# Turning the second batch's probabilities on VectorE instead of TensorE, and a table of 34 shifted due times

## The chip, the cores and the metric

The kernel runs on one core of a Trainium2 chip. The metric is the device time of one execution in microseconds (us); the figure of a kernel is the median of three runs. All parts of this document speak of that one core.

## What is computed

A causal attention over 4 batches, 12 heads, 448 positions and a head size of 64 feeds a gated feed-forward layer. Cut to what matters:

```python
def _attn_ref(q, k, v):                    # [4, 12, 448, 64], float32
    scores = np.matmul(q, k.transpose(0, 1, 3, 2)) / np.sqrt(64)
    scores = np.where(mask, -1000000000.0, scores)          # causal
    scores = scores - np.max(scores, axis=-1, keepdims=True)
    attn = np.exp(scores)
    attn = attn / (np.sum(attn, axis=-1, keepdims=True) + 1e-09)
    return np.matmul(attn, v)

def _moe_ref(x, w_gate, w_val, w_out):     # x [1792, 768], w_gate, w_val [768, 1536], w_out [1536, 768]
    gate = 1.0 / (1.0 + np.exp(-(x @ w_gate)))
    return gate * (x @ w_val) @ w_out
```

## The kernel before

**The work.** The heads are taken in pairs: six pairs for each batch, 24 in all. A pair is loaded (`load`, `load_v`), its scores are computed on TensorE, the row minimum, exponential, sum and division follow on VectorE, ScalarE and GpSimd, and the probabilities, which have the query in the partition, are turned so that the key is in the partition. The turned tile `pt` is then multiplied by V, and the result is split in a high and a low part (`features`). A batch's six results are the input of the feed-forward layer. Batches 0 and 1 go through it one by one ("units" 0 and 1, `unit_items`, matmuls at L600, three of them for each product of 128 rows, since every operand is a high and a low part); batches 2 and 3 go through it together at the end (`pair_items`, L813, the "pair stage").

**Two ways to turn a pair.** The narrow way (`score`, `trans`, `pv`) cuts queries in blocks of 112: 8 score matmuls (L283), 20 transposes on TensorE against an identity (L334), five evictions of the PSUM result into `pt` (L343 on ScalarE, L345 on VectorE; for batch 1 all five on ScalarE) and 8 matmuls with V (L358). The wide way (`wscore`, `shift`, `wpv`) cuts queries in blocks of 128: 8 score matmuls (L405), then VectorE turns 32x32 blocks within their quarter of the partitions (seven operations at L455, one at L458), and two transfers bring the blocks to the right quarter: one writes the tile to a DRAM buffer `pd` (L463, 1 MB), four read it back into `pt` (L466, a quarter each). 20 matmuls with V follow (L483). A constant, `WIDE`, tells how many batches are narrow: batches 0 and 1 before. In the wide way the tile that VectorE writes is a part of `room`, the buffer that also takes the loads of the weights in unit 0.

**Weights.** In unit 0 each of the 36 weight tiles comes from the input as 64-bit words (L565, into one of three parts of `room`), ScalarE and VectorE make float32 of it (L569, L571, L573), it is written to DRAM for later use (L576), and ScalarE and a second engine split it in a high and a low part (L581, and L583 on VectorE for 34 of the 36 tiles). In unit 1 a tile is read back from DRAM (L578) and split by ScalarE and GpSimd. Three buffers at each step (`room`, `wr`, and the high and low parts) let the loads run ahead of TensorE.

**What sets the order.** Every step is an operation of a plan (`Plan.op`) with an engine, a cost and a due time. The main loop runs through the feed-forward products in their order and drops attention steps between them at fixed fractions of the way; the due time is a running sum of costs. `Plan.order` first pulls the due time of each operation forward to that of its successors, then lists the operations engine by engine: of those that are ready, the one with the earliest due time goes first. The engines execute the lists in order. All DMAs are issued by SyncE (SP), also in the order of the list.

Of the kernel before, what the change touches and what calls it, by code (L numbers as in the profile page):

```python
# [8 lines left out]
F32 = mybir.dt.float32  # L9
# [10 lines left out]
PTW = 2 * 10 * QB  # L20
# [7 lines left out]
HP = H // 2  # L28

LAG = 1  # L30
WIDE = 2
PAIR = 2
TURN, SPREAD = 0.95, 0.85
ORDER = "1256743"
# [1 line left out]
EARLY = 2  # L36
WC = 512
EV = ((1, 3, 4), (0, 1, 2, 3, 4), (1, 3, 4), (1, 3, 4))
BUFS = dict(w64=3, wd=2, wr=3, ws=3, sm=4, raw=3, pt=3, gt=5, vr=2, st=4)
LAT, LOOK, SLACK = 0.04, 0.06, 0.2  # L40
AFTER = dict(DVE=0.09, ACT=0.1, PL=0.03)

REBIAS, SIGN = 2.0 ** -112, 2.0 ** 32


class Buf:
# [35 lines left out]
class Plan:  # L84
# [60 lines left out]
    def order(self):  # L145
        for o in reversed(self.ops):
            d = min((s.due - s.cost - SLACK for s in o.succs), default=1e9) - o.extra
            o.due = d if o.due is None else min(o.due, d)
        free = {}
        shared = 0.0  # L150
        queue = {}
        for o in self.ops:
            o.left = len(o.preds) + len(o.after)
            o.ready = 0.0
            queue.setdefault(o.eng, [])
            free[o.eng] = 0.0
            if not o.left:
                queue[o.eng].append(o)
        done = []
        while True:  # L160
            best = None
            for e, q in queue.items():
                if q:
                    t = max(free[e], min(o.ready for o in q))
                    if best is None or t < best[0]:
                        best = (t, e)
            if best is None:
                break
            t, e = best
            q = queue[e]  # L170
            o = min((o for o in q if o.ready <= t + LOOK), key=lambda o: (o.due, o.n))
            q.remove(o)
            start = max(t, o.ready, shared if o.lock else 0.0)
            end = start + o.cost
            if o.lock:
                shared = end
            free[e] = end
            done.append((start, o.n, o))
            for s in o.succs:
                s.left -= 1  # L180
                s.ready = max(s.ready, end + o.extra + (LAT if s.eng != e or e != "PE" else 0.0))
                if not s.left:
                    queue[s.eng].append(s)
            for s in o.then:
                s.left -= 1
                s.ready = max(s.ready, start)
                if not s.left:
                    queue[s.eng].append(s)
        assert len(done) == len(self.ops)
        done.sort(key=lambda x: x[:2])  # L190
        return [o for _, _, o in done]
# [3 lines left out]
def kernel(  # L195
# [7 lines left out]
    nc = tc.nc  # L203
    plan = Plan()
# [10 lines left out]
    dma = lambda b: b / 355e3 + 0.03  # L215
# [11 lines left out]
    def part(n, i):  # L227

        lo = i * n
        p = Part(room, lo, n, Gone([q for q in parts if q.lo < lo + n and lo < q.lo + q.n]))  # L230
        parts.append(p)
        return p
# [212 lines left out]
    def shift(n):  # L445

        j = pairs[n]
        j["pt"] = pt = new("pt", [128, PTW], F32, BUFS["pt"])
        tb = part(4 * WC, n % 2)
        tv = lambda: tb.t.rearrange("p (r n) -> p r n", r=4)  # L450
        plan.op("PL", 0.2, lambda: nc.gpsimd.memset(tv()[:, 2:4, WC - 32:WC], 0.0), [], [(tb, "zero")])
        for z, i in [(z, i) for i in range(3) for z in range(2)] + [(0, 3)]:
            sm, o, c, at = j["sm"][z], woff(i), min(i + 1, 3), z * 192 + ioff(i) if i < 3 else 384
            r = [(sm, (i, z))] if i < 3 else [(sm, (i, 0), (i, 1))]
# [4 lines left out]
            out=tv()[:, 0:2, WC - 32:WC],  # L459
            in_=sm.t[:, woff(3) + 384:woff(3) + 448].rearrange("p (r j) -> p r j", j=32)),  # L460
            [(j["sm"][0], (3, 0), (3, 1))], [(tb, "end")])
        pd = new("pd", [128, 4 * WC], F32, 2, bass.MemoryType.DRAM)
        plan.op("SP", dma(128 * 4 * WC * 4), lambda: nc.sync.dma_start(out=pd.t, in_=tb.t),  # L463
                [(tb, "zero", "end", *[(z, i) for z in range(2) for i in range(3)], (0, 3))], [(pd,)], extra=4.2)
        for r in range(4):
            plan.op("SP", dma(32 * 4 * WC * 4), lambda r=r: nc.sync.dma_start(  # L466
# [41 lines left out]
    def att_steps(seq, wide):  # L508

        L = []  # L510
        for m in range(len(seq) + LAG + 1):
            n, c, d = (seq[e] if 0 <= e < len(seq) else None for e in (m, m - LAG, m - LAG - 1))
            if n is not None:
                L.append((0, lambda due, n=n: load(n)))
# [182 lines left out]
    def pair_inputs():  # L697
# [7 lines left out]
                halves(xa[k], *T[p, i])  # L705
        rest = {p: [] for p in "56743"}
        for p, tags in (("5", (("raw", 2),) * 3), ("6", (("sm", 2),) * 3), ("7", (("pt", 5), ("vr", 1))),
                        ("4", (("pt", 5),)), ("3", (("pt", 5),))):
            for tag, n in tags:
                rest[p] += cells(tag, n, F32R, BUFS[tag])  # L710
        a, b = cells("sm", 2, F32R, BUFS["sm"])
# [293 lines left out]
    now -= 3.0  # L1005
    last = [PAIR * HP + k for k in range(HP)] + [(PAIR + 1) * HP + k for i in range(KH) for k in (i, KH + i)]
    att = []
    for seq, wide, lo, hi in ((range(HP, 2 * HP), False, 0.0, TURN), (last, True, TURN, 1 + SPREAD)):
        steps = att_steps(seq, wide)
        pace = [a[-1] if len(a) == 3 else a[0] for a in steps]  # L1010
        da = 0.0
        for (c, f, *_), w in zip(steps, pace):
            att.append((c, f, half * (lo + (hi - lo) * da / sum(pace))))
            da += w
# [27 lines left out]
def _lay(q, k, v, moe_w_gate, moe_w_val, moe_w_out):  # L1042
# [2 lines left out]
    qkt = np.concatenate([q.transpose(0, 1, 3, 2), k.transpose(0, 1, 3, 2)], axis=3).reshape(B * HP, 128, 2 * S)  # L1045
    vt = np.zeros((B * HP, 128, NB, 2, D), v.dtype)
    vp = v.reshape(B * HP, 2, S, D)
    m = WIDE * HP
    vt[:m, :QB] = vp[:m].reshape(m, 2, NB, QB, D).transpose(0, 3, 2, 1, 4)
    for c in range(NB):  # L1050
        x = vp[m:, :, WQ * c:WQ * c + WQ]
# [34 lines left out]
```

## Time and profile before

| | before |
|---|---|
| median of three runs | 653.56 us (653.43 to 654.2) |
| the profiled execution | 654.04 us, its span 652.3 us, granted clock 0.994 |
| TensorE busy | 642.1 us (98%) |
| VectorE, ScalarE, GpSimd busy | 445.5, 359.4, 323.3 us |
| DMA, mean over the span | 210 GB/s |

The profile takes all its times from the start of the span; 1.7 us of the execution lie outside it. Four stretches are told apart below: the opening with batch 0's attention (0 to 62 us), unit 0 with batch 1's attention (62 to 223), unit 1 with the attention of batches 2 and 3 (223 to 417), and the pair stage. "DMA share" is the mean share of time in which the 16 DMA engines were busy. The names of the engines in the rows: PE is TensorE, PEld its weight load, DVE is VectorE, ACT is ScalarE, POOL is GpSimd, SP is SyncE.

### The profile page before, as it was taken

Reading aid. Unit: us, or ns where it says so; the run is one execution under the profiler, and the core shown is the slowest. Engines: PE = TensorE matmul, PEld = TensorE weight load, DVE = VectorE, ACT = ScalarE, POOL = GpSimd, SP = SyncE. Lnnn points to the kernel's source line nnn. Section 1 sums busy time; section 2 is a strip of 40 time slices with the busy share of each in tenths; the row PEclk is TensorE's granted clock in tenths of the full one; section 3 lists DMA queues with packets and bytes.
Section 4 is the critical chain, followed back from the end, with each engine's and each line's share of the span. In section 5 each row is a group of like instructions: output and inputs, shape, how many; then the busy total and the mean of one; then the engine's idle time right before and its main releaser. Section 6 shows DMA issues by size and latency. Waiting matters only on the chain.

```text
span 652.3 us, 10853 instructions
## 1 busy us (share of the span) xinstructions
PE 642.1 (98%) x3726; PEld 539.9 (83%) x3726; DVE 445.5 (68%) x999; ACT 359.4 (55%) x815; POOL 323.3 (50%) x352
## 2 busy tenths in 40 slices
PE   6999999999999999999999999999999999999997
PEld 4566887888888778778787899999999999999997
DVE  4776987878774376556565975647764459999852
ACT  6887777767664456555465645443343434556520
POOL 3751653241520277577666766756665657700300
PEclk9899999999999999999999999999999999999999
DMA  7379599877886369998989895767532322344321
GB/s 269 120 243 327 193 305 324 264 262 260 275 295 227 118 216 270 296 303 258 280 277 293 242 308 186 227 243 242 178 114 78 114 76 73 121 134 152 98 80 70
DMA packets 46678, 137.15 MB, mean 210 GB/s; under 512 B 5152, under 2 KB 8736, under 8 KB 45088
## 3 DMA queue, kind: packets, MB, share of 16 engines
q1 hardware_dynamic: 46624, 136.47, 64.0%
q8 instruction: 29, 0.48, 0.3%
q14 instruction: 25, 0.20, 0.1%
HBM read 99.48 MB, written 36.96 MB: 209 GB/s over the span
## 4 chain that ended last, share of the span: by engine, by line
PE 95%; DMA 2%; ACT 2%; SPq 0%; DVE 0%; POOL 0%; issue 0%; DVEq 0%
PE m L600 40%; PE m L813 19%; PE s L813 10%; PE t L813 7%; PE t L334 4%; PE s L283 4%; PE m L358 3%; PE m L483 3%; PE s L405 3%; DMA raw<-in_qkt_dram 2%; ACT sm L300 1%; PE t L405 1%; PE s L358 1%; POOL wl L583 0%; SPq L466 0%; ACT sm L426 0%
## 5 line engine op out<-in xcount | busy, mean ns | idle before, releaser
L767 POOL TENSOR_TENSOR wl<-room,wh 128x384 fp32r<-128x384 f32 x84 | 96.7, 1174 | 55.2 <-ACT wh L766 55.0
L600 PE MATMUL m<-xh,wh 128*128 128x448 f32 x288 | 109.8, 381 | 0.0
L600 PE MATMUL m<-xh,wl 128*128 128x448 f32 x288 | 105.3, 365 | 0.0
L600 PE MATMUL m<-xl,wh 128*128 128x448 f32 x288 | 105.2, 365 | 0.0
L583 POOL TENSOR_TENSOR wl<-wr,wh 128x768 fp32r<-128x768 f32 x38 | 74.4, 1961 | 54.0 <-ACT wh L581 53.4
L321 POOL TENSOR_SCALAR sm<-sm,r 112x112 f32<-112x112 f32 (+1 forms) x92 | 62.6, 701 | 77.4 <-DVE r L308 71.4
L581 ACT CAST wh<-wr 128x768 fp32r<-128x768 f32 x72 | 59.6, 830 | 30.7 <-PE m L600 19.6
L600 PEld LDWEIGHTS m<-xh,wh 128*128 128x128 f32 x288 | 54.1, 188 | 20.3 <-issue 13.3
L766 ACT CAST wh<-room 128x384 fp32r<-128x384 f32 x84 | 39.6, 512 | 54.2 <-POOL wl L767 15.9
L426 ACT ACTIVATE sm<-sm,mn 128x128 f32<-128x128 f32 (+3 forms) x84 | 43.9, 524 | 43.3 <-DVE mn L420 43.3
L600 PEld LDWEIGHTS m<-xh,wl 128*128 128x128 f32 x288 | 54.1, 188 | 4.5
L600 PEld LDWEIGHTS m<-xl,wh 128*128 128x128 f32 x288 | 54.2, 188 | 3.7
L300 ACT ACTIVATE sm<-sm,mn 112x112 f32<-112x112 f32 (+3 forms) x96 | 49.8, 521 | 9.8 <-DVE mn L296 9.4
L600 PE MATMUL m<-gh,wh 128*128 128x448 f32 x144 | 53.9, 374 | 0.0
L441 POOL TENSOR_SCALAR sm<-sm,r 128x256 f32<-128x256 f32 (+3 forms) x84 | 42.7, 525 | 21.7 <-DVE r L436 12.4
L583 DVE TENSOR_TENSOR wl<-wr,wh 128x768 fp32r<-128x768 f32 x34 | 36.2, 1065 | 24.2 <-ACT wh L581 23.9
L600 PE MATMUL m<-gh,wl 128*128 128x448 f32 x144 | 52.6, 366 | 0.0
L600 PE MATMUL m<-gl,wh 128*128 128x448 f32 x144 | 52.6, 365 | 0.0
L455 DVE STREAM_TRANSPOSE room<-sm 128x384 f32<-128x384 f32 (+2 forms) x84 | 35.1, 448 | 19.1 <-POOL sm L441 17.9
L630 POOL TENSOR_TENSOR gl<-gt,gh 128x448 fp32r<-128x448 f32 x24 | 30.4, 1268 | 34.2 <-ACT gh L629 34.2
L813 PE MATMUL m<-pt,wh 128*128 128x448 f32 x150 | 44.7, 366 | 0.0
L420 DVE CUSTOM_DVE_ANT_0 sm<-s,mask 128x128 f32<-128x128 f32 (+1 forms) x72 | 29.2, 440 | 21.5 <-PE s L405 20.9
(165 smaller groups left out, 1488.9 us busy)
## 6 DMA issues: line engine op xcount, KB each, us to landing
room<-in_wp_dram SPq DMA_DIRECT2D x36, 768.0 KB, 6.6
wr<-wdram SPq DMA_DIRECT2D x45, 384.0 KB, 5.0
room<-wdram SPq DMA_DIRECT2D x45, 384.0 KB, 3.6
wdram<-wr SPq DMA_DIRECT2D x36, 384.0 KB, 7.1
pd<-room SPq DMA_DIRECT2D x12, 1024.0 KB, 6.9
pt<-pd SPq DMA_DIRECT2D x48, 256.0 KB, 5.7
raw<-in_qkt_dram SPq DMA_DIRECT2D x23, 448.0 KB, 6.2
vr<-in_vt_dram SPq DMA_DIRECT2D x24, 256.0 KB, 6.1
```

The source lines that it names most:

```text
L300: plan.op("ACT", act(ne, 0, 1) + 0.01, lambda z=z, sm=sm, i=i, ne=ne, off=off: nc.scalar.activation(out=sm.t[:QB, off:off + ne], in_=sm.t[ ...
L321: plan.op("PL", 0.24 + w / 1200, lambda args=args: nc.gpsimd.tensor_scalar(**args()), [(r_,)], [(sm, a)])
L426: plan.op("ACT", act(ne, 0, 1) + 0.01, lambda z=z, sm=sm, i=i, ne=ne, off=off: nc.scalar.activation(out=sm.t[:, off:off + ne], in_=sm.t[:, ...
L441: plan.op("PL", 0.24 + w / 1200, lambda sm=sm, i=i, o=o, w=w, z=z: nc.gpsimd.tensor_scalar(out=sm.t[:, o:o + w], in0=sm.t[:, o:o + w], sca ...
L455: plan.op("DVE", dve(128 * c) + 0.03, lambda sm=sm, i=i, o=o, c=c, at=at: nc.vector.transpose(out=tv()[:, :, at:at + 32 * c].rearrange("p ...
L581: plan.op("ACT", act(768), lambda: nc.scalar.copy(hi_.t, t.t), [(t,)], [(hi_,)])
L583: plan.op(eng, cost, lambda: at.tensor_tensor(out=lo_.t, in0=t.t, in1=hi_.t.bitcast(F32), op=ALU.subtract), [(t,), (hi_,)], [(lo_,)], lock ...
L600: nc.tensor.matmul(out=ps.t[:, :S], lhsT=a.t[:, k, :], rhs=b.t if isinstance(b, Buf) else b(), start=(first and z == 0), stop=(last and z ...
L630: plan.op("PL", 1.11, lambda: nc.gpsimd.tensor_tensor(out=gl.t[:, jj], in0=gg.t, in1=gh.t.bitcast(F32), op=ALU.subtract), [(gg,), (gh,)], ...
L766: plan.op("ACT", act(w), lambda: nc.scalar.copy(f(hi_.t), x()), [(src, at)], [(hi_, e)])
L767: plan.op("PL", 0.97, lambda: nc.gpsimd.tensor_tensor(out=f(lo_.t), in0=x(), in1=f(hi_.t).bitcast(F32), op=ALU.subtract), [(src, at), (hi_ ...
L813: nc.tensor.matmul(out=ps.t[:, :S], lhsT=a.t[:, kw, :], rhs=b.at, start=bool(first and z == 0), stop=bool(last and z == 2), skip_group_che ...
```

## The change

The six pairs of batch 1 now go the wide way: `WIDE` counts pairs and is 6, and the plan's list of attention sequences has the wide form for pairs 6 to 11. While batch 1 is worked on, `room` is full of weights, so for these pairs VectorE writes into a buffer of its own, `tb`, of which there is one; the number of `pt` buffers falls from 3 to 2 to make room for it, and the operand tiles of product "3" in the pair stage, which used a `pt` buffer, use `tb`. `NUDGE` adds a time to the due time of 34 operations after the due times have been pulled forward. V is laid out for the wide form from pair 6 on.

```diff
-WIDE = 2
+WIDE = 6
...
-BUFS = dict(w64=3, wd=2, wr=3, ws=3, sm=4, raw=3, pt=3, gt=5, vr=2, st=4)
+BUFS = dict(w64=3, wd=2, wr=3, ws=3, sm=4, raw=3, pt=2, gt=5, vr=2, st=4, tb=1)
...
+NUDGE = {
+    21: 2.7, 40: -0.7, 42: 1.8, 69: -0.8, 288: 3.1, 289: 3.1, 399: 2.1, 405: 2.1, 414: 2.1, 415: 2.1, 452: 2.1,
...
+}
...
+        for n, x in NUDGE.items():
+            self.ops[n].due += x
...
-        tb = part(4 * WC, n % 2)
-        tv = lambda: tb.t.rearrange("p (r n) -> p r n", r=4)
+        tb = part(4 * WC, n % 2) if j["b"] >= PAIR else new("tb", [128, PTW], F32)
+        at_ = lambda: tb.t[:, :4 * WC]
+        tv = lambda: at_().rearrange("p (r n) -> p r n", r=4)
...
-        plan.op("SP", dma(128 * 4 * WC * 4), lambda: nc.sync.dma_start(out=pd.t, in_=tb.t),
+        plan.op("SP", dma(128 * 4 * WC * 4), lambda: nc.sync.dma_start(out=pd.t, in_=at_()),
...
-                        ("4", (("pt", 5),)), ("3", (("pt", 5),))):
+                        ("4", (("pt", 5),)), ("3", (("tb", 5),))):
...
-    for seq, wide, lo, hi in ((range(HP, 2 * HP), False, 0.0, TURN), (last, True, TURN, 1 + SPREAD)):
+    for seq, wide, lo, hi in ((range(HP, WIDE), False, 0.0, 0.03), (range(WIDE, 2 * HP), True, 0.03, TURN), (last, True, TURN, 1 + SPREAD)):
...
-    m = WIDE * HP
+    m = WIDE
```

In the rows below the changed kernel's lines stand nine or ten higher: L414, L465, L473, L476 and L493 are the wide form's L405, L455, L463, L466 and L483 of before, L575 and L586 are L565 and L576, L610 is L600.

SyncE's list in unit 0, at the loads of the 11th to 14th weight before and the 13th to 16th now (`room<-in_wp_dram` is a weight's load, `wdram<-wr` its write back, `raw` the queries and keys of a pair, `vr` its values). Before:

```order
L565 DMA room<-in_wp_dram 128x1536
L576 DMA wdram_1343<-wr 128x768
L565 DMA room<-in_wp_dram 128x1536
L576 DMA wdram_1381<-wr 128x768
L263 DMA vr<-in_vt_dram 128x512
L565 DMA room<-in_wp_dram 128x1536
L576 DMA wdram_1426<-wr 128x768
```

Now:

```order
L575 DMA room<-in_wp_dram 128x1536
L586 DMA wdram_1195<-wr 128x768
L473 DMA pd<-tb 128x2048
L575 DMA room<-in_wp_dram 128x1536
L586 DMA wdram_1270<-wr 128x768
L266 DMA raw<-in_qkt_dram 128x896
L476 DMA pt<-pd 32x4x512 x4
L575 DMA room<-in_wp_dram 128x1536
```

A pair's write to `pd` and its four reads now stand between the loads of weights, six times between the 13th load and the last.

TensorE's list in unit 0, at a step of a pair; the L600 rows between are feed-forward products of which one is shown. Before:

```order
L358 MATMUL m<-pt,vr 64x448 x2
L358 MATMUL m<-pt,vr 64x336 x2
L358 MATMUL m<-pt,vr 64x224 x2
L358 MATMUL m<-pt,vr 64x112 x2
L283 MATMUL s<-raw 112x112 x2
L283 MATMUL s<-raw 112x224 x2
L600 MATMUL m<-xh_679,wh 128x448
...
L334 MATMUL t<-ident,sm 112x112 x4
L283 MATMUL s<-raw 112x336 x2
L334 MATMUL t<-ident,sm 112x112 x4
...
L283 MATMUL s<-raw 112x448 x2
L334 MATMUL t<-ident,sm 112x112 x8
```

Now:

```order
L493 MATMUL m<-pt,vr 64x128 x12
L493 MATMUL m<-pt,vr 64x64 x8
L414 MATMUL s<-raw 64x448 x2
L610 MATMUL m<-xh_764,wh 128x448
...
L414 MATMUL s<-raw 128x128 x2
L414 MATMUL s<-raw 128x256 x2
L414 MATMUL t<-raw 128x384 x2
```

The transposes (L334) of batch 1 are gone, 120 in all; a pair's step is scores and one burst with V.

VectorE's list in unit 0 now, beside the next weights (L581, L583 and L593 are L571, L573 and L583 of before, L637 is the gate of a feed-forward tile); before, only the weights and the softmax of a pair stood here:

```order
L465 STREAM_TRANSPOSE tb<-sm 128x4x32
L465 STREAM_TRANSPOSE tb<-sm 128x2x4x32 x2
L593 TENSOR_TENSOR wl<-wr,wh 128x768
L465 STREAM_TRANSPOSE tb<-sm 128x3x4x32
L581 TENSOR_SCALAR wr<-wd 128x768
L465 STREAM_TRANSPOSE tb<-sm 128x3x4x32
L583 SCALAR_TENSOR_TENSOR wr<-room,wr 128x768
L465 STREAM_TRANSPOSE tb<-sm 128x3x4x32
L468 STREAM_TRANSPOSE tb<-sm 128x2x32
```

The eight block transposes of a pair are interleaved with the conversion of the next weight.

## Rows read from the trace of the kernel before

**Rows 1.** Windows by stage; busy PE, PEld, DVE, ACT, POOL, clock, DMA share, GB/s.
```profile
62.00:223.00 161.00, 161.00 (x898) 132.41 (x896) 117.80 (x211) 107.42 (x220) 55.54 (x63) 1.00 0.77 260
223.00:417.00 194.00, 192.97 (x1342) 159.69 (x1339) 125.77 (x412) 105.59 (x270) 130.84 (x146) 1.00 0.83 257
572.00:652.30 80.30, 76.70 (x377) 70.35 (x375) 57.81 (x86) 33.27 (x56) 7.12 (x5) 1.00 0.31 106
```

**Rows 2.** Windows of the feed-forward matmuls (L600): length, PE busy (count), clock, DMA.
```profile
62.00:223.00 161.00, 126.58 (x588) 1.00 0.77 260
223.00:417.00 194.00, 143.29 (x674) 1.00 0.83 257
```

**Rows 3.** Chain that ended last, in order of time: start, length, what.
```profile
103.38 0.91 PE t L334 x8
...
168.18 2.04 PE m L358 x16
...
277.49 1.93 PE m L483 x40
...
395.41 22.08 PE m L600 x108
```

**Rows 4.** Windows of score matmuls: L283 up to 62, L405 up to 223.
```profile
0.00:62.00 62.00, 20.83 (x108) 9.84 (x108) 0.94 0.67 232
...
62.00:223.00 161.00, 0.54 (x6) 0.52 (x8) 1.00 0.77 260
```

**Rows 5.** DMA issues of the page: count, size of each, us to landing.
```profile
room<-in_wp_dram SPq DMA_DIRECT2D x36, 768.0 KB, 6.6
...
pd<-room SPq DMA_DIRECT2D x12, 1024.0 KB, 6.9
```

**Rows 6.** Windows of the DMA alone: length, clock, share, GB/s.
```profile
84.00:112.00 28.00, 1.00 0.96 319
97.00:107.00 10.00, 1.00 0.98 319
244.00:248.00 4.00, 1.00 1.03 230
248.00:252.00 4.00, 1.00 1.03 400
```

**Rows 7.** SyncE's queue by time: start, length, line, transfer, count.
```profile
84.28 0.33 SPq L565 DMA_DIRECT2D room<-in_wp_dram  x1
...
240.11 1.80 SPq L466 DMA_DIRECT2D pt<-pd  x4
...
246.78 0.32 SPq L463 DMA_DIRECT2D pd<-room  x1
```

**Rows 8.** Windows of L600 from the start: how many were issued by then.
```profile
0.00:115.00 115.00, 47.52 (x214) 0.97 0.74 254
0.00:225.80 225.80, 136.64 (x630) 0.98 0.74 251
```

**Rows 9.** Groups by line: what turns a landed weight into matmul operands.
```profile
L569 ACT ACTIVATE wd<-room 128x768 f32<-128x768 f32 x36 | 32.8, 914 | 7.4 <-DMA room<-in_wp_dram 6.6 <-DVE wr L571 0.5
...
L571 DVE TENSOR_SCALAR wr<-wd 128x768 int32<-128x768 int32 x36 | 25.0, 698 | 4.0 <-ACT wd L569 3.2
L573 DVE SCALAR_TENSOR_TENSOR wr<-room,wr 128x768 int32<-128x768 int32 x36 | 39.7, 1104 | 0.8
...
L581 ACT CAST wh<-wr 128x768 fp32r<-128x768 f32 x72 | 59.6, 830 | 30.7 <-PE m L600 19.6 <-issue 6.6 <-POOL sm L441 1.6
...
L583 DVE TENSOR_TENSOR wl<-wr,wh 128x768 fp32r<-128x768 f32 x34 | 36.2, 1065 | 24.2 <-ACT wh L581 23.9
```

**Rows 10.** Groups by line: VectorE's share of a turned pair, with its idle time.
```profile
L455 DVE STREAM_TRANSPOSE room<-sm 128x384 f32<-128x384 f32 (+2 forms) x84 | 35.1, 448 | 19.1 <-POOL sm L441 17.9 <-DMA raw<-in_qkt_dram 0.7
...
L420 DVE CUSTOM_DVE_ANT_0 sm<-s,mask 128x128 f32<-128x128 f32 (+1 forms) x72 | 29.2, 440 | 21.5 <-PE s L405 20.9
...
L434 DVE TENSOR_SCALAR r<-sum 128x4 f32<-128x4 f32 (+2 forms) x36 | 8.7, 252 | 9.2 <-ACT sm L426 8.5
```

More of the change, by code (lines that the diff above doesn't have):

```diff
@@ L510, in att_steps @@
         L = []
-        for m in range(len(seq) + LAG + 1):
+        for m in range(len(seq) + LAG + 1 if seq else 0):
             n, c, d = (seq[e] if 0 <= e < len(seq) else None for e in (m, m - LAG, m - LAG - 1))
```

3 rows, old and new, of the table NUDGE are left out of this document.

## The prediction, made before the changed kernel was run

> **What bounds the kernel now.** I read the windows by stage first. From 62 to 223 us TensorE is busy for 161.0 of 161.0 us, from 223 to 417 for 192.97 of 194, in the last stage for 76.70 of 80.3 [rows 1]. Nothing makes it wait in the stage that the change touches, so the stage lasts as long as TensorE's list, and a shorter list shortens it for as long as the others keep up. In the same row VectorE is busy for 117.8 us and the DMA engines for 0.77 of the time: those are the two that could fail to keep up. For what an attention step costs on TensorE I then read the feed-forward matmuls of each stage [rows 2] and the chain [rows 3]; for the DMA, the issues, the windows of stretches in which its engines are never idle, and SyncE's queue [rows 5 to 7]; for how far the loads run ahead, the time of a load against the count of matmuls issued [rows 7, 8]; and for the way from a landed weight to its first matmul, and for VectorE, the groups by line [rows 9, 10].
>
> **What leaves TensorE.** 108 feed-forward matmuls in an undisturbed stretch take 22.08 us [rows 3], 0.2044 each. The 588 of the stage from 62 to 223 make 120.2 us; the other 40.8 are attention [rows 1, 2]. Of these 0.5 us are the first wide scores of batch 2, while 12 of batch 1's score matmuls came before 62 us: 108 stand there, 96 of them batch 0's, at 20.83/108 us each, 2.3 us [rows 4]. So six narrow pairs cost 42.6 us, 7.1 each: 20 transposes at 0.91 us for eight are 2.28, the burst with V 2.04 [rows 3], the scores the other 2.78. In the next stage 674 matmuls make 137.8 us and 1.0 us is idle; 55.2 remain, with the 0.5 from before 55.7 for twelve wide pairs, 4.64 each [rows 1, 2]: 1.93 with V [rows 3], 2.71 for the scores. The change saves 2.46 us a pair, **14.7 us** in all, if TensorE never waits.
>
> **What is added to the DMA.** Each pair writes 1,024 KB to `pd` and reads as much back [rows 5]; six pairs make 6.3 MB each way. From 244 to 248 us, while the reads issued at 240.1 are under way, the engines are full (1.03) and move 230 GB/s; from 248 to 252, after the write issued at 246.8, they are full and move 400 [rows 6, 7]. So the reads take 27.4 us of all engines, the writes 15.7, and that stage is already at 0.77 of 161. The count is made where it is densest, from the 13th weight's load to the last. In the new order 23 loads of 768 KB, 24 write backs of half that size, three `raw` (448 KB), four `vr` (256 KB) and two output tiles (224 KB) are issued between them: 30.4 MB. At the rate of the stretch that holds almost only such transfers, 319 GB/s at a share of 0.96 [rows 6], thus 332, they take 91.6 us. With the six writes and the 24 reads: **134.7 us** of DMA, if the engines are never idle.
>
> **What TensorE allows for it.** The 13th weight's first matmul is the 217th, at about 115.5 us, the 36th weight's is the 631st, at 225.8 [rows 8]. Before the 217th the list of before has 28 score matmuls of batch 1, 40 transposes and two bursts with V, 18.4 us by the prices above; the new one has 24 wide scores and one burst, 10.1. Before the 631st it is 44.6 us (all of batch 1 and six wide scores) against 32.6 (62 wide scores, six bursts). So without a wait TensorE would come to them at 107.2 and 213.8, 106.6 us apart. The loads run ahead: the 13th is issued at 84.3 and lands some 6.6 us later [rows 5, 7], 24.6 us before its use. I take the same lead for the changed kernel, since the same three buffers at each step set it. From landing to matmul a weight needs five operations, 0.91, 0.70, 1.10, 0.83 and 1.07 us [rows 9], with the signals between them about 5 us (my estimate from that sum of 4.6). So 19.6 us of the lead can be spent. The DMA needs 134.7 - 106.6 = 28.1 us more than TensorE over this stretch, 8.5 more than the lead has: **TensorE waits some 8.5 us** before the end of unit 0, and the wait is not won back, since the later stages leave TensorE no idle time. 14.7 - 8.5 = 6.2 us are gained.
>
> The price of 134.7 us is for a share of 1.00. A queue that is always full reads 1.03, and with that it is 131 us and a wait of 5; the densest ten microseconds in the loads read 0.98 and the densest 28 read 0.96 [rows 6]: 137 or 140 us, and a wait of 11 or 14. I take 1.00, between the full queue and the densest row of weights, because there is now always something to issue.
>
> The Trainium skill (DMA: Bandwidth & Descriptors, Bandwidth) gives about 358 GB/s as the limit of one core's transfers with DRAM. By that figure alone the stretch's 43.0 MB would take an estimated 120 us, TensorE would not wait, and the sum would be the whole gain. The rows disagree in both directions, with 400 GB/s for the writes and 230 for the reads of a full queue [rows 6].
>
> **What is added elsewhere.** VectorE gets the block transposes, 35.1 us for twelve pairs, and three pieces of row sums instead of one, 8.7 for twelve [rows 10]: about 3.7 us a pair, 22 us, hidden as long as VectorE has idle time: 117.8 + 22 = 140 of 146 us. ScalarE loses 30 evictions and GpSimd is busy for 55.5 of 161 us [rows 1]: no cost. SyncE issues a write and four reads more for a pair, 0.3 and 1.8 us [rows 7], 13 us over the stage, in time in which it otherwise waits for a buffer of `room`. Two `pt` buffers instead of three, and one `tb`, cost nothing while a pair's step, some 20 us, is longer than the write's 6.9 us to landing [rows 5]; if the queue is late, the next pair's transposes wait for `tb`, which the second rival prices. Of the table I count nothing: the idle time that it could remove in the last stage is 3.6 us [rows 1], and I know no row that tells which of it.
>
> **The sum.** The profiled execution took 654.04 us, span 652.3 and 1.7 around it. 654.04 - 14.7 + 8.5 = 647.8; the median of before is 0.5 lower, so the median to expect is **647.5 us**. A measurement of this kernel tells 0.2%, 1.3 us, from no change.
>
> **Rivals.**
> *The whole gain.* The DMA engines take more than I think, or the loads start from a longer lead: no wait, 653.6 - 14.7 = 638.9. For it: nothing in the rows stalls TensorE at a share of 0.83 over a stage [rows 1]. Against: full windows are seen at 230 GB/s. The page's figure above would lead here. 0.20.
> *SyncE leaves the queue empty, and the change is slower.* It issues in order, and the reads of `pd` can only be issued when the write has landed; what stands behind them, the next weight's load among it, waits too. If the engines stay at 0.92, between the loads' 0.96 and the 0.83 of the stage in which every pair goes this way [rows 1, 6], the stretch takes 146.4 us, TensorE waits 20.2 and the time is 653.6 + 5.5 = 659. It decides from a share of 0.956 down, where the wait equals the gain. 0.20.
> *VectorE becomes the bound.* In the wide stage it waited 20.9, 17.9 and 8.5 us for twelve pairs for scores, for GpSimd and for sums [rows 10]; for six that is 24. With 140 of work the stage would last 164 us, 3 longer than now: 656. Against: of its present idle time 23.9 us are waits for casts [rows 9], which are held back by full buffers and vanish when it is late. 0.08.
> *Nothing measurable.* The wait comes to 13.4 to 16 us: the engines at about 0.95. 0.12.
>
> **How the numbers follow.** The forecast's own case, a gain of 1.3 to 11 us, has 0.40. Faster by over 0.2%: 0.40 + 0.20 = 0.60; within it 0.12; slower 0.20 + 0.08 = 0.28. The range reaches from just above the whole gain, 640, to the second rival's 659; outside lie about 2 in 10.
>
> **What would show it.** In the profile after: 120 transposes fewer on TensorE and about 14.7 us less attention; from some 80 us to unit 0's end a DMA share of 0.95 or more; waits of TensorE, or of its weight loads, for the weights' high and low parts (L591 to L593), several microseconds, all before about 230 us, growing towards the end of unit 0; no new wait behind that. It is wrong if TensorE does not wait there, if it waits for `pt` rather than weights, if the DMA share stays near 0.9 while TensorE waits, or if VectorE is busy without a gap.

## The result, and the profile after

The changed kernel takes 642.83 us (median of four runs, 641.15 to 644.19), the kernel before 653.49 in the same comparison: a ratio of 0.9831, 95% interval [0.9808, 0.9853]. The forecast was 647.5 us, in a range from 640 to 659: 10.7 us were gained where 6.2 were forecast. The profiled execution of the changed kernel took 644.19 us, its span is 642.5; it is the slowest of the four, 1.4 us above their median.

Windows by stage of the changed kernel, with the columns of [rows 1]:

```profile
62.00:211.00 149.00, 145.11 (x870) 123.86 (x868) 124.41 (x287) 89.00 (x187) 50.91 (x60) 0.99 0.99 340
211.00:404.00 193.00, 192.35 (x1369) 160.05 (x1368) 124.80 (x403) 106.21 (x263) 129.81 (x146) 1.00 0.88 279
571.00:642.50 71.50, 68.03 (x335) 62.55 (x333) 50.41 (x73) 27.71 (x47) 7.25 (x5) 1.00 0.29 100
```

In the first row, unit 0, the DMA share went from 0.77 to 0.99 and TensorE is no longer busy without a gap: 3.9 of 149 us are idle. What TensorE waited for in the whole span, longest first (waiter, line, releaser; us in total, times, longest):

```profile
PE s L292 <- DMA raw<-in_qkt_dram: 3.8, 1, 3.8
PE m L493 <- DMA pt<-pd: 3.6, 2, 2.9
PE m L610 <- DVE xl L381: 0.9, 1, 0.9
```

The first is the start of the program. The second is new: two bursts with V (L493) that wait for a turned tile. The chain of waits around the longer one, in order of time (start, length, what):

```profile
156.48 6.14 DMA wdram<-wr
162.62 0.57 DVE tb L465
163.18 0.84 DVE wr L583
164.02 0.49 DVE tb L465
164.51 0.14 DVE tb L468
...
164.70 9.43 DMA pd<-tb
...
175.06 7.50 DMA pt<-pd
182.55 0.93 issue
183.48 3.59 PE m L493 x40
```

VectorE finishes turning at 164.65, the write to DRAM takes 9.43 us where the median of before was 6.9 [rows 5], the reads take 7.50, and the burst starts at 183.48. It then lasts 3.59 us instead of 1.93 [rows 3]. Three windows of the DMA and the clock, the second and third around this burst (columns of [rows 1]):

```profile
100.00:120.00 20.00, 20.00 (x132) 16.88 (x131) 17.37 (x44) 12.98 (x28) 9.39 (x10) 1.00 1.01 362
...
180.00:200.00 20.00, 17.05 (x106) 15.47 (x105) 12.21 (x20) 8.18 (x11) 2.16 (x3) 0.91 1.03 367
184.00:186.00 2.00, 2.00 (x22) 2.00 (x20) 0.26 (x1) 0.81 (x1) 0.00 (x0) 0.50 1.00 409
```

The granted clock is 1.00 before the wait, 0.91 on the mean of the 20 us that hold it, and 0.50 from 184 to 186 us: most of the burst ran at the lower of the two levels, 1.2 instead of 2.4 GHz. So this one wait cost 2.95 + 1.66 = 4.6 us. A weight takes longer to land too, 8.5 us at the median instead of 6.6 [rows 5]:

```profile
room<-in_wp_dram SPq DMA_DIRECT2D x36, 768.0 KB, 8.5
pt<-pd SPq DMA_DIRECT2D x72, 256.0 KB, 6.5
```

and the operations that turn a landed weight into operands, with their idle time as in [rows 9], show where the waiting moved:

```profile
L579 ACT ACTIVATE wd<-room 128x768 f32<-128x768 f32 x36 | 32.7, 912 | 29.1 <-DMA room<-in_wp_dram 29.0
...
L593 DVE TENSOR_TENSOR wl<-wr,wh 128x768 fp32r<-128x768 f32 x34 | 34.0, 999 | 8.1 <-ACT wh L591 8.1
```

ScalarE now waits 29.0 us for weights to land (before 6.6), and VectorE only 8.1 for ScalarE's casts (before 23.9). SyncE's own waits from 62 to 211 us (waiter, releaser; us in total, times, longest) show that the loads depend on VectorE as well:

```profile
SPq L575 <- DVE wr L583: 39.2, 15, 6.9
SPq L473 <- DVE tb L468: 18.0, 6, 5.2
```

SyncE waits 39.2 us for VectorE's last step on a weight, which frees a part of `room`, before it issues another load, and 18.0 us for VectorE to finish turning a pair. So even at a DMA share of 0.99 a load often starts only when VectorE lets it, and where VectorE is later the DMA is idle more (turning twice, below: a share of 0.93).

**Where the time went.** For each kernel the table takes TensorE's list, prices it with the prediction's prices (0.2044 us for a feed-forward matmul, 0.91/8 for a transpose, 2.78/8 and 2.71/8 for a narrow and a wide score, 2.04/8 and 1.93/20 for the matmuls with V) and subtracts this from the time that passed in the profiled execution. What is left is time lost to waits and to a lower clock, true to about 1 us, since a few records are missing. The columns count feed-forward matmuls: 217 is the 13th weight's first, 631 the 36th's.

| profiled execution, us | first one starts | lost, 1 to 216 | lost, 217 to 630 | lost, 631 to pair stage | pair stage | span |
|---|---|---|---|---|---|---|
| before | 45.4 | -1.1 | -0.5 | 1.7 | 235.0 | 652.3 |
| changed | 42.4 | 0.6 | 5.7 | 1.2 | 234.9 | 642.5 |

By this list 14.8 us of work left TensorE. The prices are the forecast's own, so the table tests them only where TensorE has no gap: there the column reads -0.5 (before) and, further below, -0.4 (three pairs) and -0.5 (both reliefs), so that they hold to about 0.5 us in 110. Between the 217th and the 630th matmul 6.2 us more are lost than before, and 1.7 up to the 216th; 0.5 are won back later. The first feed-forward matmul comes 3.0 us earlier, and only 0.7 of that is work that moved behind it: 2.3 us were gained in the opening. Together -14.8 + 6.2 + 1.7 - 0.5 - 2.3 = -9.7, and the span fell by 9.8.

### The profile page after: what moved, and what is told of

It reads as the page before. It is cut to its first block, busy times and chain, and to the rows that moved or that the text cites. A ratio compares the mean times of both kernels' runs of the same rounds, so it can differ in the third digit from the quotient of the medians.

```text
span 642.5 us, 10964 instructions
## 1 busy us (share of the span) xinstructions
PE 628.4 (98%) x3750; PEld 534.9 (83%) x3750; DVE 454.0 (71%) x1071; ACT 340.4 (53%) x773; POOL 316.5 (49%) x352
## 4 chain that ended last, share of the span: by engine, by line
PE 82%; DMA 11%; ACT 3%; DVE 2%; issue 1%; POOL 1%; SPq 1%; ACTq 0%; DVEq 0%; POOLq 0%
PE m L610 32%; PE m L823 19%; PE s L823 10%; PE t L823 7%; PE m L493 4%; PE s L414 4%; DMA room<-in_wp_dram 3%; DMA pd<-tb 3%; DMA pt<-pd 2%; ACT sm L309 2%; PE t L414 2%; PE s L292 1%; DMA pd<-room 1%; DMA wdram<-wr 1%; PE t L343 1%
## 5 line engine op out<-in xcount | busy, mean ns | idle before, releaser
L777 POOL TENSOR_TENSOR wl<-room,wh 128x384 fp32r<-128x384 f32 x84 | 94.7, 1150 | 56.4 <-ACT wh L776 56.4
L610 PE MATMUL m<-xh,wh 128*128 128x448 f32 x288 | 109.3, 380 | 0.9 <-DVE xl L381 0.9
L610 PE MATMUL m<-xl,wh 128*128 128x448 f32 x288 | 105.3, 365 | 0.0
L610 PE MATMUL m<-xh,wl 128*128 128x448 f32 x288 | 105.3, 365 | 0.0
L450 POOL TENSOR_SCALAR sm<-sm,r 128x384 f32<-128x384 f32 (+3 forms) x126 | 78.7, 641 | 51.5 <-DVE r L445 43.9
L435 ACT ACTIVATE sm<-sm,mn 128x128 f32<-128x128 f32 (+3 forms) x126 | 65.9, 524 | 48.2 <-DVE mn L429 43.2
L593 POOL TENSOR_TENSOR wl<-wr,wh 128x768 fp32r<-128x768 f32 x38 | 72.6, 1915 | 36.8 <-ACT wh L591 36.2
L610 PEld LDWEIGHTS m<-xh,wh 128*128 128x128 f32 x288 | 54.1, 188 | 25.4 <-issue 17.6
L610 PEld LDWEIGHTS m<-xh,wl 128*128 128x128 f32 x288 | 54.1, 188 | 4.4
L429 DVE CUSTOM_DVE_ANT_0 sm<-s,mask 128x128 f32<-128x128 f32 (+1 forms) x108 | 44.3, 439 | 18.5 <-PE s L414 17.6
L610 PEld LDWEIGHTS m<-xl,wh 128*128 128x128 f32 x288 | 54.2, 188 | 3.7
L610 PE MATMUL m<-gh,wh 128*128 128x448 f32 x144 | 53.6, 372 | 0.0
L610 PE MATMUL m<-gl,wh 128*128 128x448 f32 x144 | 52.7, 366 | 0.0
L610 PE MATMUL m<-gh,wl 128*128 128x448 f32 x144 | 52.7, 366 | 0.0
L579 ACT ACTIVATE wd<-room 128x768 f32<-128x768 f32 x36 | 32.7, 912 | 29.1 <-DMA room<-in_wp_dram 29.0
L465 DVE STREAM_TRANSPOSE room<-sm 128x384 f32<-128x384 f32 (+2 forms) x84 | 34.6, 445 | 18.0 <-POOL sm L450 17.7
L493 PEld LDWEIGHTS m<-pt,vr 128*64 128x64 f32 x720 | 35.1, 142 | 9.1 <-issue 6.7
L493 PE MATMUL m<-pt,vr 128*64 128x128 f32 (+1 forms) x720 | 37.5, 261 | 3.6 <-DMA pt<-pd 3.6
```

The costliest lines, as they stand in the source:

```text
L429: plan.op("DVE", dve(ne), lambda z=z, y=y, sm=sm, i=i, o=o, ne=ne, off=off, s0=s0, at=at: nc.vector.tensor_tensor_reduce(out=sm.t[at, off: ...
L435: plan.op("ACT", act(ne, 0, 1) + 0.01, lambda z=z, sm=sm, i=i, ne=ne, off=off: nc.scalar.activation(out=sm.t[:, off:off + ne], in_=sm.t[:, ...
L450: plan.op("PL", 0.24 + w / 1200, lambda sm=sm, i=i, o=o, w=w, z=z: nc.gpsimd.tensor_scalar(out=sm.t[:, o:o + w], in0=sm.t[:, o:o + w], sca ...
L465: plan.op("DVE", dve(128 * c) + 0.03, lambda sm=sm, i=i, o=o, c=c, at=at: nc.vector.transpose(out=tv()[:, :, at:at + 32 * c].rearrange("p ...
L493: nc.tensor.matmul(out=vp.t[64 * z:64 * z + 64, i * WQ:i * WQ + rows(i)], lhsT=v.t[:, c, z], rhs=src, start=(c == 0), stop=(c == i))
L593: plan.op(eng, cost, lambda: at.tensor_tensor(out=lo_.t, in0=t.t, in1=hi_.t.bitcast(F32), op=ALU.subtract), [(t,), (hi_,)], [(lo_,)], lock ...
```

## The experiments

The medians of before on the chips used were 653.5 to 654.8 us, so kernels of different comparisons are set side by side by their ratios to it. After the text of each run its "lost" column for matmuls 217 to 630 is given, worked out as above.

**The pairs without the table.**

```diff
-NUDGE = { ... }
+NUDGE = {}
```

> The changed kernel with an empty table, nothing else. If the six pairs carry the gain and the table only smooths the order, the time stays within 3 us of the changed kernel's 642.8. If the table carries it (its first entries reorder the opening, where the changed kernel's granted clock is 1.00 instead of 0.94), the time goes back by more than that, to 648 or above.

649.86 us, ratio 0.9933 [0.9899, 0.9966]: the six pairs alone gain some 4 us, and the table is worth the difference to 0.9831, about 1.0% or 6.7 us. The ten runs of this kernel lie between 645.5 and 654.7 us, wider than those of the changed kernel. Lost, in its one profiled execution: 9.5 us. The chain of waits of this kernel at its longest wait:

```profile
167.19 7.42 DMA pd<-tb
...
176.83 9.28 DMA vr<-in_vt_dram
186.12 0.23 issue
186.34 3.38 PE m L488 x40
```

It is the same burst (here L488) as in the changed kernel's chain. The write to `pd` is issued 2.5 us later, at 167.19 instead of 164.70, `vr` is issued behind the four reads that wait for that write, and TensorE waits 4.09 us and again takes more than 3 us for the burst. The pair stage takes 234.7 us without the table and 234.9 with it, so the table's entries there moved nothing that can be measured.

**Half of the traffic.** Batch 1 writes half of `tb` and reads two quarters; zeros stand for the others, so the result leaves those quarters out.

```diff
-nc.sync.dma_start(out=pd.t, in_=at_())
+nc.sync.dma_start(out=pd.t[:, :w_], in_=tb.t[:, :w_])          # w_ = 2 * WC for batch 1
+if few and r > 1:
+    if r == 2: nc.gpsimd.memset(pt.t[64:128, :4 * WC], 0.0)
+    return
```

> The changed kernel, in which batch 1's pairs write only half of their turned tile to DRAM and read only two of the four quarters back; GpSimd fills the other two quarters of pt with zeros, so batch 1's result leaves them out. That is 3.1 MB less each way, some 21 us of all DMA engines by the rates of the full queue. If the DMA is what makes TensorE wait in unit 0, the waits of 0.9 and 2.9 us and the stretch at a clock of 0.83 behind the second go, and the time falls by 4 to 6 us to 637 to 639. If VectorE or the order sets the wait, it stays at 642 to 643.

641.16 us, ratio 0.9792 [0.9767, 0.9817], some 2.5 us faster than the changed kernel, though the two intervals touch. The fall of 4 to 6 us that was expected did not come. Lost: 1.2 us.

**More traffic.** Each of batch 1's pairs copies four times 128 KB from DRAM to DRAM, which nothing waits for.

```diff
+if j["b"] < PAIR:
+    nc.sync.dma_start(out=idle.tile([128, 256], F32, ...), in_=vt[n][:, :256])   # four times a pair
```

> The changed kernel with four extra copies of 128 KB from DRAM to DRAM for each pair of batch 1, each issued behind one of its reads; nothing reads them. 3.1 MB, some 9 us of all engines at 340 GB/s. If the DMA engines are the bound of unit 0, TensorE's wait grows by about that much and the time is 649 to 654. If they have room left, the time moves by less than 2 us.

649.93 us, ratio 0.9919 [0.9886, 0.9952], some 5.8 us slower than the changed kernel. Lost: 13.1 us. With these two the loss moves with the traffic in both directions, with no instruction changed on TensorE, VectorE or ScalarE. That the volume alone sets it is not shown: SyncE issues two transfers fewer for a pair in the first and four more, of 0.50 us each, in the second, where the DMA moves as much as in the changed kernel, at a somewhat lower share (columns of [rows 1]):

```profile
62.00:211.00 149.00, 142.56 (x854) 120.70 (x853) 121.39 (x281) 86.18 (x178) 51.29 (x59) 0.99 0.96 341
```

The 24 copies take 12 us of SyncE's time in issues, and a run that adds issues without bytes was not made.

**The buffers alone**, in the kernel before:

```diff
-BUFS = dict(... pt=3, ...)
+BUFS = dict(... pt=2, ..., tb=1)
-("3", (("pt", 5),))
+("3", (("tb", 5),))
```

> The kernel before with only the change of buffers: two for pt, one for tb, and the tiles of product 3 in tb. I counted this at nothing: within 0.2% of the kernel before. If two buffers hold a pair's reads back, the time rises by 2 us or more, and the gain of the changed kernel contains that loss.

654.13 us, ratio 0.9994 [0.9975, 1.0014]: nothing, as the prediction counted. Lost: -0.5 us.

**The table without its opening.**

```diff
-    21: 2.7, 40: -0.7, 42: 1.8, 69: -0.8, 288: 3.1, 289: 3.1, 399: 2.1, ...
+    399: 2.1, ...
```

> The changed kernel with the table's first six entries (batch 0's opening and the first matmul of unit 0) taken out, the other 28 kept. Without any table the time was 649.9 us, with all of it 642.8. Theory A (the opening entries are worth the 2 us by which the first feed-forward matmul comes earlier, at 42.4 instead of 44.5 us; the other entries the rest, at the end of unit 0, where TensorE waits for the DMA): 645 us, the opening's granted clock between 10 and 20 us back at about 0.76, and the stretch from the 630th feed-forward matmul to the pair stage as short as with the whole table, 188 us. Rival B (the whole worth of the table is the opening): 649.9 us. Rival C (the opening entries do nothing): 642.8 us.

641.49 us, ratio 0.9815 [0.9792, 0.9837]: not told apart from the changed kernel, as rival C said. Yet the opening itself behaves as theory A said. Windows from 10 to 20 us, first of the changed kernel, then of this one (columns of [rows 1]; the clock stands before the DMA share):

```profile
10.00:20.00 10.00, 8.51 (x54) 4.44 (x54) 8.64 (x34) 9.09 (x30) 8.57 (x15) 1.00 0.59 233
```

```profile
10.00:20.00 10.00, 8.42 (x38) 4.57 (x38) 6.95 (x28) 8.11 (x27) 8.44 (x15) 0.69 0.52 210
```

With the six entries TensorE issues 54 matmuls in these 10 us at a granted clock of 1.00, without them 38 at 0.69, and its first feed-forward matmul comes at 43.8 instead of 42.4 us. The 1.4 us are gone by the end: this kernel lost 1.2 us in unit 0, the changed one 5.7. These are one execution each, the fastest of five here and the slowest of four there, so that a part of the difference is the spread between executions. The 28 other entries carry the table's worth, 0.9933 against 0.9815. The burst that waited 2.95 us in the changed kernel waits 1.22 here, and after this shorter wait it takes 2.00 us:

```profile
182.09 2.00 PE L493 MATMUL m<-pt,vr 128*64 128x128 f32 x40 [1.22 <-DMA pt<-pd]
```

**The opening entries alone.**

```diff
+NUDGE = {21: 2.7, 40: -0.7, 42: 1.8, 69: -0.8, 288: 3.1, 289: 3.1}
```

> The changed kernel with only the table's first six entries, the other 28 taken out. Theory A: 649.9 - 2 = 648 us, the granted clock between 10 and 20 us about 1.00, and the waits at the end of unit 0 (for vr, for the weights' high and low parts) still there. Rival B: 643 us. Rival C: 650 us.

647.73 us, ratio 0.9902 [0.9886, 0.9918]. The middle is theory A's 648, and the clock from 10 to 20 us is 1.00, but the interval overlaps that of the kernel without a table. Lost: 7.8 us. Rival B falls.

**Turning twice.** VectorE does each of batch 1's block transposes a second time.

```diff
-nc.vector.transpose(out=..., in_=...)
+for _ in range(2 if j["b"] < PAIR else 1):
+    nc.vector.transpose(out=..., in_=...)
```

> The changed kernel with every block transpose of batch 1 done twice into the same place: some 17.5 us more of VectorE (eight for a pair take 2.93 us, six pairs), no byte more for the DMA; unit 0 would have VectorE busy for some 142 of 149 us. If the DMA is what holds unit 0 (theory A), the time stays within 2 us of 642.8. If VectorE has become the bound, as one rival of the prediction says, at least half of the 17.5 us shows: 651 us or more.

654.23 us, ratio 0.9996 [0.998, 1.0011]: by the ratios 10.8 us lost of the 17.5 added. Theory A's "within 2 us" was wrong: DMA volume is not the only limit. Windows from 80 to 180 us, of this kernel (in the fastest of its twelve runs) and of the changed one (columns of [rows 1]; VectorE's busy time is the third):

```profile
80.00:180.00 100.00, 92.49 (x568) 77.31 (x567) 96.99 (x229) 58.63 (x124) 35.28 (x42) 0.97 0.93 309
```

```profile
80.00:180.00 100.00, 99.06 (x618) 84.11 (x617) 89.36 (x216) 62.27 (x132) 39.66 (x48) 1.00 1.01 337
```

With 97 of 100 us busy VectorE is the bound and the DMA share falls to 0.93; in the changed kernel VectorE is at 89 and the DMA at 1.01. Some 6.7 us of VectorE's time were free in the changed kernel, no more.

**A tile moved without DRAM.** For batch 1 `tb` goes to `pt` directly.

```diff
-one write of 1 MB to pd, four reads of 256 KB into pt
+for a in range(4):
+    nc.sync.dma_start(out=pt.t[32 * r:32 * r + 32, a * WC:a * WC + WC],
+                      in_=tb.t[32 * a:32 * a + 32, r * WC:r * WC + WC])       # for each r, 16 in all
```

> The changed kernel with batch 1's turned tile moved from tb straight into pt, 16 transfers of 32 partitions by 512 elements for each pair in place of one write to DRAM and four reads: half the bytes, and no 2 KB rows read from DRAM. If the DMA's volume holds unit 0 (theory A), the six pairs need 16 to 27 us of all DMA engines in place of 43 (6.3 MB at 400 or at 230 GB/s), more than the 7 us that TensorE lost, and the time falls to between 636 and 641 us. If the wait is one of order and latency in SyncE's queue, it stays at 643 us; if SyncE's time for issuing holds (16 issues of some 0.45 us, 7.2 us a pair in place of 2.1), it rises above 645 us.

668.68 us, ratio 1.0224 [1.0202, 1.0246], the slowest of all. SyncE's queue and a window at one such group of issues:

```profile
117.79 10.03 SPq L481 DMA_DIRECT2D pt<-tb  x16
```

```profile
117.80:127.80 10.00, 7.77 (x38) 6.69 (x36) 9.25 (x25) 6.81 (x19) 1.87 (x2) 1.00 0.39 100
```

The last theory was right. 16 issues hold SyncE for 10.03 us, 0.63 each, and as each brings only 64 KB, the DMA engines are busy for 0.39 of that time and move 100 GB/s, while weights stand behind in the queue. Half of the bytes, and 26 us more than the changed kernel, because the queue that issues became the limit. The Trainium skill (DMA: Bandwidth & Descriptors, Bandwidth) advises transfers of 1 MiB or more and gives 138 GB/s for one of 64 KB that is read from DRAM and issued by GpSimd. This run agrees with the advice; its 100 GB/s come from the spacing of SyncE's issues, and no run here measures that figure.

**Less work on VectorE.** GpSimd makes the low part of each third weight.

```diff
-("DVE", 0.87, nc.vector) if EARLY <= p < NP else ("PL", 1.8, nc.gpsimd)
+("DVE", 0.87, nc.vector) if EARLY <= p < NP and p % 3 else ("PL", 1.8, nc.gpsimd)
```

> The changed kernel with the low part of 11 of unit 0's weights made on GpSimd instead of VectorE: VectorE loses 11 x 1.0 = 11 us of its 124 from 62 to 211 us, GpSimd gains 11 x 1.9 = 21 on its 51. Turning twice (17.5 us more of VectorE) cost 11.4 us, halving the traffic gained 1.7 to 2.5. Theory D (a ring of three weights, in which a load of 8 to 10 us and VectorE's own lateness follow each other, sets the pace, so that either alone counts): VectorE earlier makes the parts of room come free earlier, and the wait before the pair stage shrinks by some 2 to 4 us: 639 to 641 us. Theory A (the DMA volume alone, VectorE with 6 us to spare): 642.8 as before. Rival E (GpSimd, slower at this step, holds TensorE's weights up, or shares its port with VectorE): above 644 us.

649.63 us, ratio 0.9914 [0.9896, 0.9932], slower than the changed kernel: rival E by the number, but not by its mechanism. TensorE waited 0.2 us for low parts made by GpSimd. What it waited for was `vr`:

```profile
175.49 0.38 SPq L575 DMA_DIRECT2D room<-in_wp_dram  x1
175.91 0.45 SPq L272 DMA_DIRECT2D vr<-in_vt_dram  x1
```

```profile
187.41 3.68 PE L493 MATMUL m<-pt,vr 128*64 128x128 f32 x40 [5.85 <-DMA vr<-in_vt_dram]
```

The planner, given other costs, put `vr` behind a `pt` read and a weight; in the changed kernel the same pair's `vr` was issued at 160.04. It landed 11.3 us after its issue. So this run says little on VectorE, and much on the order. Lost: 8.6 us, and 4.3 after the 630th matmul, where a burst waited 2.73 us for `pt` at 390 us.

**Both reliefs.** Half of the traffic, as above (two quarters left out), and each third low part on GpSimd.

> Both reliefs together: batch 1's traffic through DRAM halved (half of tb is written, two quarters are read, the other two are zeros, so the result leaves those quarters out) and the low part of 11 weights made on GpSimd. Theory D: no wait is left before the pair stage, and the whole of the 7 us comes back: 635 to 637 us. Theory A: as with half the traffic alone, 641 us. Rival E: above 642 us.

638.52 us, ratio 0.9754 [0.974, 0.9767]; theory D's 635 to 637 was a little low. Lost: -0.5 us. Windows from 62 to 211 us of this kernel and of the one with half the traffic alone (columns of [rows 1]):

```profile
62.00:211.00 149.00, 149.00 (x930) 127.30 (x929) 129.64 (x287) 92.66 (x193) 86.83 (x84) 1.00 0.92 310
```

```profile
62.00:211.00 149.00, 147.73 (x921) 125.75 (x920) 129.78 (x297) 92.87 (x190) 64.31 (x72) 1.00 0.92 305
```

TensorE is busy for 149.00 of 149 us: the whole gain, 16.3 us against before, of which 14.8 is work that left; the opening, 2.3 us earlier in the changed kernel, would cover the rest. Against half the traffic alone it is some 2.5 us, with intervals that touch, so that VectorE's part is likely rather than shown.

**Three pairs.**

```diff
-WIDE = 6
+WIDE = 9
-NUDGE = { ... }
+NUDGE = {}
-(range(HP, WIDE), False, 0.0, 0.03), (range(WIDE, 2 * HP), True, 0.03, TURN)
+(range(HP, WIDE), False, 0.0, 0.47), (range(WIDE, 2 * HP), True, 0.47, TURN)
```

> Only three of batch 1's pairs (the last three) go the wide way, no table. TensorE is relieved of 3 x 2.46 = 7.4 us, and the DMA gets 21.5 us of the 43. If unit 0 has room for half of the added load (the lead of 19.6 us covers it): 653.6 - 7.4 = 646.2 us, better than all six without a table (649.9). If the loss comes with the way itself, pair by pair, and not with a load beyond what unit 0 has room for, three pairs give half of what six gave without a table: 653.6 - 2 = 651.5 us.

648.26 us, ratio 0.9903 [0.9889, 0.9918]: 6.5 us gained with half of the pairs and no table, where all six gained 4.4; the intervals overlap, and the trace tells more. TensorE was busy without a gap from 62 to 211 us, and the column says -0.4 us lost:

```profile
62.00:211.00 149.00, 149.00 (x880) 124.72 (x880) 120.28 (x245) 96.46 (x198) 52.56 (x60) 1.00 0.89 296
```

The loss does not come with each pair; it comes with the load beyond what unit 0 has room for.

**Five pairs**, with the six opening entries.

```diff
-WIDE = 6
+WIDE = 7
-NUDGE = { ... }
+NUDGE = {21: 2.7, 40: -0.7, 42: 1.8, 69: -0.8, 288: 3.1, 289: 3.1}
-(range(HP, WIDE), False, 0.0, 0.03), (range(WIDE, 2 * HP), True, 0.03, TURN)
+(range(HP, WIDE), False, 0.0, 0.16), (range(WIDE, 2 * HP), True, 0.16, TURN)
```

> Five of batch 1's pairs wide (the first stays narrow), and of the table only the first six entries. The prediction's own count, with one pair less: the DMA needs 134.7 - 7.2 = 127.5 us between the 13th and the 36th weight, TensorE 106.6 + 2.5 = 109.1, and the lead has 19.6: no wait, and 5 x 2.46 = 12.3 us are gained. With the 2 us of the opening entries (six pairs: 649.9 without, 647.7 with them) the time is 654.2 - 12.3 - 2 = 640 us, level with all six pairs and the whole table (642.8) or just under it. If the loss grows with each pair instead (six pairs with these entries gained 6.4 us), five gain about 5.5: 648 to 649 us, with waits of TensorE near 180 us as before.

652.79 us, ratio 0.9974 [0.9956, 0.9992]; both expectations failed. The stretch that the count was made for has no wait, as it said (127.00 of 127 us; lost from 217 to 630: -0.1):

```profile
84.00:211.00 127.00, 127.00 (x771) 109.08 (x770) 102.31 (x240) 72.70 (x149) 39.64 (x49) 1.00 0.93 320
```

But 7.6 us are lost before it, up to the 216th matmul, where the one narrow pair is done. Its transposes wait for ScalarE's evictions of the transposes before them:

```profile
74.64 1.03 PE L338 MATMUL t<-ident,sm 112*112 112x112 f32 x8 [0.56 <-ACT pt L347]
79.04 0.99 PE L338 MATMUL t<-ident,sm 112*112 112x112 f32 x4 [3.37 <-ACT pt L347]
```

That the short share of unit 0 given to this pair (0.16 of the way) crowded it is argued, not shown. No experiment with the full result is faster than the changed kernel by more than the measurement tells.

| profiled execution, us | first one starts | lost, 1 to 216 | lost, 217 to 630 | lost, 631 to pair stage |
|---|---|---|---|---|
| no table | 44.5 | 0.7 | 9.5 | 2.0 |
| opening entries alone | 42.2 | 0.5 | 7.8 | 2.8 |
| table without its opening | 43.8 | 0.7 | 1.2 | 0.5 |
| half of the traffic | 42.9 | 0.6 | 1.2 | 2.1 |
| more traffic | 42.3 | 0.6 | 13.1 | 0.5 |
| turning twice | 42.1 | 0.6 | 12.5 | 0.9 |
| directly | 42.9 | 2.1 | 25.0 | 5.8 |
| less on VectorE | 43.2 | 0.5 | 8.6 | 4.3 |
| both reliefs | 42.3 | 0.6 | -0.5 | 1.6 |
| three pairs | 45.9 | -0.5 | -0.4 | 2.4 |
| five pairs | 44.9 | 7.6 | -0.1 | 2.1 |

## Why the prediction held, and where it did not

**The work that leaves TensorE** was right: 14.7 us forecast, and with all waits gone (both reliefs) the kernel gains this and little more.

**The DMA's 134.7 us and the wait of 8.5** were right in kind: the DMA share is 0.99 over the 149 us of unit 0, and TensorE loses several microseconds there. Without the table, which the sum did not count, 9.5 us are lost between the 217th and the 630th matmul, 7.8 with the opening entries, and with the whole table 5.7 in the profiled execution. That 8.5 lies among these is luck, for two terms of the sum were wrong by about as much, in opposite directions. In the changed kernel's trace, the issues of the 13th and of the 36th weight's load, the window between them (columns of [rows 1]), and the matmuls issued by two times (columns of [rows 8]):

```profile
77.43 0.33 SPq L575 DMA_DIRECT2D room<-in_wp_dram  x1
...
201.21 0.33 SPq L575 DMA_DIRECT2D room<-in_wp_dram  x1
77.43:201.21 123.78, 119.89 (x743) 102.57 (x742) 105.22 (x245) 71.44 (x146) 43.71 (x53) 0.99 1.01 342
0.00:106.40 106.40, 47.05 (x216) 1.00 0.78 268
0.00:219.20 219.20, 134.37 (x630) 0.99 0.89 305
```

The DMA took 123.8 us where the sum has 134.7, at a share of 1.01. And of the 19.6 us of lead that the sum spends only 10.9 were spent: the 13th load is issued 29.0 us before its first matmul, the 36th still 18.1 us before its own. With TensorE's work at 107.2 us (414 feed-forward matmuls, 38 wide scores and five bursts, at the table's prices) the terms as measured are 123.8 - 107.2 - 10.9 = 5.7, the loss. With the DMA's 123.8 in place of its 134.7 the prediction's sum would have had no wait at all. Read in the same way, the kernel without the table has 122.8, 104.5 and 8.6. So TensorE did not mainly wait because the weights' lead ran out; what it waited for follows below. The price came from windows of 4 us: ten-us windows of the changed kernel lie between 259 and 421 GB/s at shares near 1.00, so one window was a thin basis.

The count's other point, that a smaller load costs nothing, is shown by three pairs (-0.4) and in the same stretch by five (-0.1). What sets the pace when six pairs go this way is not settled between the DMA's volume, SyncE's issues and VectorE, which frees the buffers: more of each made the kernel slower.

By the 358 GB/s of the Trainium skill (DMA: Bandwidth & Descriptors, Bandwidth) the DMA would have taken an estimated 120 us and TensorE would not have waited. The stretch took 123.8 us at 342 GB/s, nearer to that estimate than to the sum's 134.7; TensorE waited all the same, for a tile and not for want of lead.

**The table, "counted as nothing", is the other step that failed.** It is worth about 6.7 us. The prediction looked for its worth in the 3.6 us of idle time in the pair stage, where it moved nothing. Its worth is in unit 0: in the profiled executions the 28 entries behind the opening bring the loss from 9.5 to 1.2 us, and by the medians they are worth some 7.7. Most of that was there to be removed only because the change itself puts a wait there, and a count of the kernel before, which has no such wait, could not show it. What the two chains show is that the write of a pair's tile is issued 2.5 us earlier; which single entry does it was not tried. The opening's 2.3 us (the granted clock from 10 to 20 us is 1.00 and was 0.68) are real in the trace and shorten the whole little or not at all.

**Where the wait stands.** The prediction said that TensorE would wait for the weights' high and low parts, and that it was wrong if it waited for `pt`. It did wait for `pt`, so by its own sign it was wrong here. By the chain above, both go through the same full DMA: a tile goes through it twice, write and read, 9.43 + 7.50 us and the issues between them, and so is late before a weight is, which goes through once and is three buffers ahead. Without the table `vr` was late at the same place, and then weights (1.4 us for a high part). What the prediction left out is the clock: after the wait the burst took 1.66 us longer.

**What lies beside.** Buffers: nothing, as said (0.9994). VectorE: its new work was hidden, as said, though not at 140 of 146 us: it was busy for 124.4 of 149 in unit 0 and for 89 of 100 where it is densest. That 17.5 us more work cost 10.8, and so 6.7 were free, is near the 6 that the count left, but by chance. The rival that it becomes the bound was nearer than its 0.08. SyncE: the rival's share of 0.92 did not come with a write of 1 MB and reads of 256 KB, though SyncE did wait for the writes to land, 18.0 us in the changed kernel's unit 0; with transfers of 64 KB the share fell to 0.39 while they were issued.

**The rivals.** The whole gain, 638.9, is what both reliefs give together (638.5, the opening's gain among it) and the changed kernel did not reach. An empty queue and a time above that of before came only with the direct way.

## What to carry to other kernels

When work moves from a full engine to the DMA, sum the DMA's demand over the densest stretch, by rates of the kernel's own full windows, and set it against what the full engine allows plus the lead of the loads: here that told that the DMA would be full and TensorE would wait. Its size, 8.5 us against 9.5, came out by errors of 10.9 and 8.7 us that cancel, so read each term in the trace afterwards, and not the sum alone. Then ask which transfer goes through the full queue twice, because it was late first here, and where it is issued: with the queue full, the order was worth more (6.7 us) than the pairs without it (4.4). A transfer with half of the bytes in four times as many pieces is no relief when one queue issues all.

## What was not expected of the hardware

- A wait of 2.95 us at 180 us was followed by a burst at a lower clock, 3.59 us instead of 1.93; waits of 2.30, 4.09 and 5.85 us at the same place gave 3.56, 3.38 and 3.68. After a wait of 1.22 us it took 2.00. The length of the wait alone does not decide: with less work on VectorE a burst at 390 us took 2.00 after a wait of 2.73.
- The DMA moved 340 GB/s at a share of 0.99 for 149 us, 50.7 MB, though 6.3 MB of them were reads of the kind that had shown 230 GB/s in a full window of 4 us [rows 6].
- An issue of a 32x512 tile-to-tile transfer held SyncE's queue for 0.59 us (median of 96), longer than one of a 768 KB weight, 0.33, and it landed 2.0 us after its issue (median).
